# A re-planned order: the planner counts turns of the TensorE array and the SyncE time of transposing DMAs

## The chip, the cores and the metric

One core of one Trainium2 chip runs the whole program in one launch. The metric is the time on the device in microseconds (us). Engines: PE (TensorE, matmul), DVE (VectorE), ACT (ScalarE), POOL (GpSimd) and SP (SyncE, which here issues every DMA).

## The reference

Causal attention over 4 batches, 12 heads, 448 tokens and 64 channels per head, and behind it a two-layer MLP with a squared ReLU over all 1792 tokens. All inputs and outputs are float32.

```python
scores = (1/8) * q @ k.T                 # [4, 12, 448, 448], above the diagonal -1e9
attn   = exp(scores - max) / (sum + 1e-9)
x      = (attn @ v) as [1792, 768]       # tokens by heads*channels
out    = relu(x @ w_in)**2 @ w_out       # w_in [768, 2048], w_out [2048, 768]
```

## The kernel before, in words

**Stages.** Heads go in pairs, six pairs to a batch; two heads fill the 128 channels of PE's rows. For each pair PE transposes q and k (L570), then makes the scores in four passes c = 0 to 3 of 112, 224, 336 and 448 columns, one matmul per head and pass (L594; 64 of the array's 128 rows for each head, so both heads use the array side by side: the array is *split*). DVE adds the mask and takes the row maximum (L599), ACT makes the exponentials and their sums (L603). Batch 0 is turned by PE and multiplied in float32 (L629, L641). In batches 1 to 3 (pairs 0 to 17 below) the probabilities are divided by their sum and written as two halves in float16, a high one (L397 on ACT, L399 on DVE or POOL) and the remainder (L410 on DVE; L413 and L415, two instructions, on POOL), four pieces a head, into `psrc`. There is one `psrc` per head of the pair. A transposing DMA per head turns `psrc` into `pT` (L556), and PE multiplies `pT` with v in 24 matmuls for the pair (L651, split again, by columns): the *values*. They alternate between the two heads, so all but the first wait for both heads' DMA.

**MLP.** Tokens go in eight blocks of 128 or 256. Each block has a first layer of 16 groups of 18 matmuls (L918: three products of halves, six slices of 128 rows), then relu (L929), square (L936), high half (L397) and remainder (L405) of `g`, and a second layer (L954, 48 matmuls for each 128 tokens and 384 columns), scaled by ACT (L964) and stored by SP (L968). The 128-row matmuls use the *full* array. Weights are loaded, narrowed (L721 to L736) and split into halves (L397, L399, L410) while batch 0 runs.

**The order.** No engine's order is written by hand. `Plan.add` records each operation with the engines that may do it and their modelled durations, and with a due time made from the table `PR` (base, step and an offset by kind). `Plan.order` plays the program through once on the host: each time, the engine that can start first takes the ready operation with the earliest due time; an operation with several engines goes to the one that would end it first, `PR`'s bias included. The order that results is emitted, engine by engine, and each engine executes in that order and waits by semaphores. The model knows PE's clock (`warm`), the port that DVE and POOL share (`locks`), one DMA lane (`dma_free`), and how long SP is held by an issue (`ISSUE`: 475 ns, and 650 ns for a transposing DMA, `heavy`).

Of the kernel before, what the change touches and what calls it, by code (L numbers as in the profile page):

```python
# [18 lines left out]
E23 = float(2 ** 23)  # L19
PSC = float(2 ** 14)  # L20
PR = {
    "bias_dve": 329, "bias_act": -2161, "bias_pool": -229, "T0": -215719, "RAMP": 92933, "B1": 32241, "S1": 125326,
    "B2": 1585202, "S2": 69324, "B3": -4763872, "S3": 34284, "M0": 1770315, "RATE": 0.0019, "WI0": 135987,
    "WIR": 56308, "WS0": 3823057, "WSR": -44877, "WO0": 940458, "WOR": 183845, "WT0": -466469, "WTR": 280709,
# [5 lines left out]
    "m_L2": 2404805, "m_fac": -4350124, "m_ghi": 179886, "m_glo": -223927, "m_msq": 1943718, "m_ob": 5617141,  # L30
    "m_relu": -2665863, "m_sig": 3771052, "m_sq": -634180, "m_tau": 1847951, "wi_wl": 351942, "wi_wn": -1179075,
    "wi_wq": 1731582, "wo_wl": 2402465, "wo_wn": -983095, "wo_wq": -76879, "ws_wn": 4319096, "wt_wn": 1234225,
    "a0_P.copy@act": -2272, "a0_P.copy@dve": 3583, "a0_P.nrm@act": -308, "a0_P.nrm@dve": 3448, "a0_P.nrm@pool": -1037,
    "a0_qk.copy@act": -4902, "a0_qk.copy@dve": -890, "a0_x.top@act": 4549, "a0_x.top@dve": 5350,
    "m_ghi.hi@act": -5477, "m_ghi.hi@dve": -2320, "m_ghi.hi@pool": -5555, "m_glo.lo@dve": -384,
    "m_glo.lo@pool": -5962, "m_relu.@act": -4403, "m_relu.@dve": 5641, "m_sq.@act": -2058, "m_sq.@dve": 782,
    "m_sq.@pool": -1987, "ws_wn.hi@act": -3852, "ws_wn.hi@dve": -6000, "ws_wn.hi@pool": -3283, "ws_wn.lo@dve": -212,
    "ws_wn.lo@pool": 3600, "wt_wn.hi@act": -2079, "wt_wn.hi@dve": -3096, "wt_wn.hi@pool": -1467,
# [10 lines left out]
}  # L49


# [14 lines left out]
class Plan:  # L66
    LAT = {"pe": 197.0, "dve": 150.0, "act": 145.0, "pool": 90.0, "sp": 0.0}
    OWN = {"pe": 0.0, "dve": 127.0, "act": 143.0, "pool": 90.0, "sp": 0.0}
    WINDOW = 4096 / 1.2
    ISSUE = {False: 475.0, True: 650.0}  # L70

    def __init__(self):
        self.ops = []
        self.heavy = set()
        self.last_w = {}
        self.last_r = {}
        self.rings = {}
        self.spots = {}
        self.port = []
        self.bias = []  # L80
        self.kind = []

# [62 lines left out]
    def order(self):  # L145
# [7 lines left out]
        free = {}  # L153
# [20 lines left out]
            if left[i] == 0:  # L174
                offer(i)
        done = 0
        warm, busy, edge = False, 0.0, self.WINDOW
        while done < n:
            best = None
            for strict in (True, False):  # L180
                for e, c in cand.items():
# [5 lines left out]
                    if e in ("dve", "pool"):  # L187
                        t = max(f, min(max(r, shared) if locks(i, e) else r for i, r in c.items()))
                    else:
                        t = max(f, min(c.values()))  # L190
# [22 lines left out]
            t, e, i = best  # L213
            dur = self.ops[i][0][e]
            start[i] = t
            on[i] = e
            if e == "sp":
                free[e] = t + self.ISSUE[i in self.heavy]
                s = max(dma_free, free[e] + 625.0)
                dma_free = s + dur  # L220
                end[i] = s + dur + 930.0
            else:
                if e == "pe":
                    while t >= edge:
                        warm = busy >= 0.68 * self.WINDOW or (warm and busy >= 0.41 * self.WINDOW)
                        busy, edge = 0.0, edge + self.WINDOW
                    if not warm:
                        dur *= 2.0
                    s = t
                    while t + dur >= edge:  # L230
                        busy += edge - s
                        warm = busy >= 0.68 * self.WINDOW or (warm and busy >= 0.41 * self.WINDOW)
                        s, busy, edge = edge, 0.0, edge + self.WINDOW
                    busy += t + dur - s
                free[e] = t + dur
                end[i] = t + dur
                if locks(i, e):
                    shared = t + dur - 140.0
# [35 lines left out]
def mm32_ns(n):  # L274
    return n / 0.6 + 6
# [7 lines left out]
def attention_relu2_kernel(  # L283
# [9 lines left out]
    nc = tc.nc  # L293
# [87 lines left out]
    gf = g.rearrange("p k h t -> p (k h t)")  # L381
    xf = xt[1].rearrange("p k h t -> p (k h t)")

    def one(e, ns, fn, reads, writes, due, heavy=False, port=False):
        i = plan.add({e: ns}, fn, reads, writes, due, port=port)
        if heavy:
            plan.heavy.add(i)
        return i

    def hi(n, out, in_, scale, reads, writes, due):  # L390
# [153 lines left out]
    def halves(n, src, rr, rkey, pT):  # L544
# [3 lines left out]
        for c in range(NCH):  # L548
# [4 lines left out]
            hi(w, lambda half=half: half(0), from_, lambda c=c: rr(c, c + 1), [(src, c), rkey], [pk + (c, 0)], due)  # L553
            lo(w, lambda half=half: half(1), from_, lambda c=c: rr(c, c + 1), lambda half=half: half(0),
               [(src, c), rkey, pk + (c, 0)], [pk + (c, 1)], due, [(src, c)])
        one("sp", 2500, lambda e: nc.sync.dma_start_transpose(out=pT.ap, in_=ps.rearrange("p a d -> p (a d)")),  # L556
            [pk + (c, z) for c in range(NCH) for z in range(2)] + ["pads"], [pT], due, True)

    def pair(i):
        b, pr = divmod(i, NPAIR)  # L560
# [24 lines left out]
        for c in range(NCH):  # L585
# [7 lines left out]
                    r = slice(j * D, (j + 1) * D)  # L593
                    nc.tensor.matmul(out=ss[j].ap[0:P, 0:w], lhsT=q32.ap[r, c * P:w], rhs=k32.ap[r, 0:w], start=True, stop=True)  # L594

            one("pe", mm32_ns(w) + 95, scores, [q32, k32], ss, due)
            for j in range(2):
                s, due = ss[j], ("a", 2 * i + j + 0.05 * c, "sc")
                one("dve", dve_ns(w, 1, 1) - 10, lambda e, c=c, w=w, s=s, j=j: nc.vector.tensor_tensor_reduce(  # L599
# [55 lines left out]

        due = ("a", 2 * i + 1, "val")
        if b:
            one("pe", 1600, values16, [(vp, 0), (vp, 1)] + pT, [pv], due)
        else:
            one("pe", 2050, values, raws[2][1] + [(p_, a) for p_ in pT for a in range(0, NB10, 4)], [pv], due)  # L660
        due = ("a", 2 * i + 1, "x")
        o = 64 * (b % 2)
        xs = xt[b % 2][:, pr]
# [387 lines left out]
```

## Time and profile before

| what | us |
|---|---|
| median of 3 runs | 713.72 (710.70 to 714.43) |
| the profiled execution | 715.77 |
| its span, first to last instruction | 714.0 |
| PE busy | 658.6 (92% of the span) |
| ACT, DVE, POOL busy | 423.7, 325.8, 266.9 |

The profiled execution took 715.77 us by the device's own time, 1.8 us more than its span; it lies 0.3% above the median of the runs. All stretches and rows below are from this one execution, in microseconds from its start. Busy shares are means over stages with different limits, so they are read by stage in what follows.

### The profile page before, as it was taken

What the parts mean: (1) busy time and instruction counts of PE and PEld (TensorE: products, weight loads), DVE (VectorE), ACT (ScalarE), POOL (GpSimd) and SP (SyncE); (2) the same over time, 40 slices, a digit from 0 to 9 for tenths busy, and PEclk for the clock granted to TensorE, in tenths of its full rate; (3) what the DMA queues carried; (4) which work ended last, traced back from release to release, by engine and by line L of the source; (5) the groups of instructions that cost most, each with busy time, mean ns of one, the idle gap of its engine ahead of it and who ended that gap; (6) DMA issues with size and microseconds to landing.
All of it is one profiled execution on the core that took longest, in us unless ns stands there. A gap on an engine that the chain in (4) does not pass through costs nothing.

```text
span 714.0 us, 13829 instructions
## 1 busy us (share of the span) xinstructions
PE 658.6 (92%) x5182; PEld 465.0 (65%) x5182; DVE 325.8 (46%) x933; ACT 423.7 (59%) x1211; POOL 266.9 (37%) x382
## 2 busy tenths in 40 slices
PE   5877776799999899999999999999989899999998
PEld 3554544587666666787757756767656778776864
DVE  4999799889884555316320235123633110200000
ACT  2788978789876774774546664348645524414410
POOL 4232333215410326468348654447545202202200
PEclk9876767689999999999999999999999899999999
DMA  9997767545476664443365345435451300000000
GB/s 249 290 279 283 262 236 264 133 91 110 86 134 135 135 125 99 96 85 81 80 127 115 66 97 108 85 59 98 96 96 47 61 2 12 12 12 23 12 12 33
DMA packets 184866, 79.04 MB, mean 111 GB/s; under 512 B 173792, under 2 KB 179680, under 8 KB 184800
## 3 DMA queue, kind: packets, MB, share of 16 engines
q1 hardware_dynamic: 184800, 78.17, 45.7%
q8 instruction: 40, 0.66, 0.4%
q14 instruction: 26, 0.21, 0.1%
HBM read 45.81 MB, written 5.51 MB: 72 GB/s over the span
## 4 chain that ended last, share of the span: by engine, by line
PE 66%; DVE 14%; DMA 9%; POOL 5%; issue 3%; ACT 2%; SPq 1%; POOLq 0%; ACTq 0%; DVEq 0%
PE bank L918 27%; PE bank L954 23%; DMA pT<-psrc 7%; PE bank L594 5%; PE bank L651 4%; DVE bank L599 3%; PE bank L570 2%; DVE wo L724 2%; POOL p L413 2%; POOL psrc L415 2%; PE bank L641 2%; DVE wi L724 1%; DMA xt<-in_moe_w_out_dram 1%; DVE psrc L410 1%; DVE wo L721 1%
## 5 line engine op out<-in xcount | busy, mean ns | idle before, releaser
L918 PE MATMUL bank<-xt,wi 128*128 128x256 f16 (+1 forms) x2304 | 235.5, 262 | 0.0
L954 PE MATMUL bank<-wo,g 128*128 128x384 f16 x1344 | 228.8, 326 | 0.0
L918 PEld LDWEIGHTS <-wi 128*128 128x128 f16 x2304 | 201.5, 99 | 36.6 <-issue 14.3
L954 PEld LDWEIGHTS <-g 128*128 128x128 f16 x1344 | 128.2, 98 | 89.9 <-issue 10.0
L405 POOL TENSOR_TENSOR g<-g,g 128x256 f16<-128x256 f32 (+1 forms) x128 | 82.0, 650 | 197.2 <-ACT g L397 101.7
L599 DVE CUSTOM_DVE_ANT_0 bank<-bank,mask 112x112 f32<-112x112 f32 (+1 forms) x192 | 82.3, 472 | 128.8 <-PE bank L594 126.7
L603 ACT ACTIVATE p<-bank,nm 112x112 f32<-112x112 f32 (+1 forms) x192 | 93.3, 491 | 65.8 <-DVE nm L599 38.4
L594 PE MATMUL bank<-kT,qT 64*112 64x112 f32 (+3 forms) x384 | 78.0, 464 | 7.4 <-ACT p L603 4.4
L929 ACT ACTIVATE r<-bank 128x256 f32<-128x256 f32 (+1 forms) x128 | 45.0, 354 | 58.9 <-PE bank L918 58.0
L964 ACT ACTIVATE ob<-bank,fac 128x384 f32<-128x384 f32 x28 | 16.2, 579 | 82.5 <-PE bank L954 82.4
L397 ACT ACTIVATE psrc<-p,nm 112x448 f16<-112x448 f32 (+3 forms) x140 | 63.6, 524 | 0.4 <-ACT p L603 0.2
L415 POOL TENSOR_TENSOR psrc<-p,psrc 112x112 f16<-112x112 f32 (+3 forms) x76 | 53.8, 707 | 6.3
L936 ACT ACTIVATE g<-r 128x256 f32<-128x256 f32 (+1 forms) x122 | 46.8, 388 | 11.7 <-POOL g L405 7.0
L413 POOL TENSOR_SCALAR p<-p,nm 112x112 f32<-112x112 f32 (+3 forms) x76 | 43.5, 572 | 26.8 <-ACT psrc L397 26.8
L397 ACT ACTIVATE g<-g 128x256 f16<-128x256 f32 (+1 forms) x123 | 46.0, 386 | 10.7 <-PE bank L954 8.9
L594 PEld LDWEIGHTS bank<-kT,qT 64*112 64x112 f32 x384 | 31.4, 180 | 27.8 <-ACT p L603 10.9
L651 PE MATMUL bank<-pT,vp 112*64 112x336 f16 (+3 forms) x432 | 34.7, 295 | 12.2 <-DMA pT<-psrc 12.2
L410 DVE SCALAR_TENSOR_TENSOR psrc<-p,nm,psrc 112x336 f16<-112x336 f32 (+3 forms) x68 | 37.7, 592 | 10.5 <-ACT psrc L397 7.0
L651 PEld LDWEIGHTS <-vp 112*64 112x64 f16 x432 | 24.6, 114 | 24.3 <-issue 19.6
L603 ACT ACTIVATION_READ_ACCUMULATOR p<-bank,nm 112x1 f32 x192 | 38.1, 198 | 0.0
L736 POOL TENSOR_TENSOR wo<-wo,l 128x512 int32<-128x512 int32 (+1 forms) x16 | 20.0, 1253 | 44.3 <-DVE wo L724 9.2
L629 PE MATMUL bank<-ident,p 112*112 112x112 f32 x120 | 28.2, 394 | 6.2 <-ACT p L530 4.3
(120 smaller groups left out, 641.3 us busy)
## 6 DMA issues: line engine op xcount, KB each, us to landing
raw<-in_moe_w_out_dram SPq DMA_DIRECT2D x8, 768.0 KB, 5.1
xt<-in_moe_w_out_dram SPq DMA_DIRECT2D x8, 768.0 KB, 5.4
xt<-in_moe_w_in_dram SPq DMA_DIRECT2D x11, 512.0 KB, 6.2
out_dram<-ob SPq DMA_DIRECT2D x28, 192.0 KB, 2.0
raw<-in_moe_w_in_dram SPq DMA_DIRECT2D x9, 512.0 KB, 6.6
vn<-in_v_dram SPq DMA_DIRECT2D x18, 224.0 KB, 3.9
raw<-in_q_dram SPq DMA_DIRECT2D x36, 112.0 KB, 2.4
raw<-in_k_dram SPq DMA_DIRECT2D x36, 112.0 KB, 2.7
```

What stands on the lines that cost most here:

```text
L397: nc.scalar.activation(out=o, in_=i, func=ACTF.Copy, scale=s)
L405: return plan.add({"dve": dve_ns(n), "pool": pool2_ns(n)}, lambda e: engines[e].tensor_tensor(out=out(), in0=in_(), in1=top(), op=ALU.subt ...
L413: nc.gpsimd.tensor_scalar(out=in_(), in0=in_(), scalar1=scale(), scalar2=1.0, op0=ALU.mult, op1=ALU.mult)
L415: nc.gpsimd.tensor_tensor(out=out(), in0=in_(), in1=top(), op=ALU.subtract)
L594: nc.tensor.matmul(out=ss[j].ap[0:P, 0:w], lhsT=q32.ap[r, c * P:w], rhs=k32.ap[r, 0:w], start=True, stop=True)
L599: one("dve", dve_ns(w, 1, 1) - 10, lambda e, c=c, w=w, s=s, j=j: nc.vector.tensor_tensor_reduce(out=s.ap[0:P, 0:w], in0=s.ap[0:P, 0:w], in ...
L603: one("act", act_ns(w, True, 1, True), lambda e, c=c, w=w, b0=b0, s=s, j=j: nc.scalar.activation(out=p32[j].ap[:, b0:b0 + c + 1, :].rearra ...
L651: nc.tensor.matmul(out=pv.ap[j * D:(j + 1) * D, kc * P:S], lhsT=vp.ap[:, hv, vb:vb + D], rhs=pT[j].ap[0:P, hp * NSL + x:hp * NSL + x + w, ...
L918: nc.tensor.matmul(out=h.ap[:, 0:n], lhsT=wi_hl(ci, hw)[:, ms], rhs=x[:, kd, hx, off:off + n], start=(kd == 0 and hw == 0 and hx == 0), st ...
L929: nc.scalar.activation(out=r.ap[:, 0:n], in_=h.ap[:, 0:n], func=ACTF.Relu)
L936: nc.scalar.activation(out=g32.ap[:, 0:n], in_=r.ap[:, 0:n], func=ACTF.Square)
L954: nc.tensor.matmul(out=o.ap[:, 0:HALF], lhsT=g[:, kf, hg, tt * 128:(tt + 1) * 128], rhs=wo_hl(kf, hw)[:, hh * HALF:(hh + 1) * HALF], start ...
```

## The change

The table `PR` is replaced as a whole (all 150 numbers or so; two are shown), and the model that turns it into an order is changed in three places: a turn of the array between full and split use adds 93 ns, a transposing DMA holds SP for 3500 ns in place of 650 and its lane for 500 in place of 2500, and the values' modelled time is 1550 in place of 1600. What is computed, the tiles, and the buffers stay as they are.

```diff
-    "bias_dve": 329, "bias_act": -2161, "bias_pool": -229, "T0": -215719, "RAMP": 92933, "B1": 32241, "S1": 125326,
+    "bias_dve": 1722, "bias_act": -3826, "bias_pool": 4333, "T0": -530296, "RAMP": 129571, "B1": 324428, "S1": 232955,
...
-    ISSUE = {False: 475.0, True: 650.0}
+    ISSUE = 475.0
+    TURN = 93.0
...
-                free[e] = t + self.ISSUE[i in self.heavy]
+                free[e] = t + self.wait.get(i, self.ISSUE)
...
+                    if (i in self.tiled) != split:
+                        split = not split
+                        dur += self.TURN
...
-        one("sp", 2500, lambda e: nc.sync.dma_start_transpose(out=pT.ap, in_=ps.rearrange("p a d -> p (a d)")),
-            [pk + (c, z) for c in range(NCH) for z in range(2)] + ["pads"], [pT], due, True)
+        one("sp", 500, lambda e: nc.sync.dma_start_transpose(out=pT.ap, in_=ps.rearrange("p a d -> p (a d)")),
+            [pk + (c, z) for c in range(NCH) for z in range(2)] + ["pads"], [pT], due, 3500.0)
...
-            one("pe", mm32_ns(w) + 95, scores, [q32, k32], ss, due)
+            one("pe", mm32_ns(w) + 95, scores, [q32, k32], ss, due, tiled=True)
...
-            one("pe", 1600, values16, [(vp, 0), (vp, 1)] + pT, [pv], due)
+            one("pe", 1550, values16, [(vp, 0), (vp, 1)] + pT, [pv], due, tiled=True)
```

The new file has seven lines more from L80 on, so that L556 of before reads L563 after, L594 reads L601, L651 reads L658, L918 reads L925, L954 reads L961, L968 reads L975, and so on. Every engine's order is different from its first rows on. By kind, the counts of instructions differ in three ways: all 128 remainders of `g` (L405) go from POOL to DVE; of the 144 remainders of the probabilities POOL has 47 in place of 76, those of batches 1 and 2 being all on DVE and those of batch 3, but for one, on POOL; and of 18 remainders of v DVE has 16 in place of 3.

PE around the values of pair 16, the last but one: the matmuls, one row where equal kinds follow each other. Before:

```order
L594 MATMUL bank_119<-kT,qT 112x448
...
L918 MATMUL bank_131<-xt_147,wi 128x128
...
L954 MATMUL bank_143<-wo,g 128x384
...
L954 MATMUL bank_139<-wo,g 128x384
...
L594 MATMUL bank_119<-kT,qT 112x336
...
L651 MATMUL bank_115<-pT,vp 64x448
```

The same place of the change:

```order
L601 MATMUL bank_119<-kT,qT 112x448
...
L925 MATMUL bank_135<-xt_147,wi 128x256
...
L872 MATMUL bank_135<-sq,ones_b 128x128
...
L961 MATMUL bank_139<-wo,g 128x384
...
L925 MATMUL bank_131<-xt_147,wi 128x128
...
L601 MATMUL bank_119<-kT,qT 112x336
...
L658 MATMUL bank_115<-pT,vp 64x448
```

Between the last score pass of pair 16 and its values stood 72 matmuls of the first layer (128 columns), 54 of the second and three score passes of pair 17; now 36 of the first layer at 256 columns, 72 at 128, 48 of the second, seven small ones and the same three passes.

SP at the end of attention, from the transposing DMAs of pair 16 on (`psrc_150` and `psrc_151` are the two heads' `psrc`). Before:

```order
L556 DMA_TRANSPOSE pT<-psrc_150 128x26x112
L556 DMA_TRANSPOSE pT<-psrc_151 128x26x112
L968 DMA out_dram<-ob 128x384 x3
L556 DMA_TRANSPOSE pT<-psrc_150 128x26x112
L556 DMA_TRANSPOSE pT<-psrc_151 128x26x112
L968 DMA out_dram<-ob 128x384 x10
```

The same place of the change:

```order
L563 DMA_TRANSPOSE pT<-psrc_150 128x26x112
L975 DMA out_dram<-ob 128x384
L563 DMA_TRANSPOSE pT<-psrc_151 128x26x112
L975 DMA out_dram<-ob 128x384
L563 DMA_TRANSPOSE pT<-psrc_150 128x26x112
L975 DMA out_dram<-ob 128x384 x2
L563 DMA_TRANSPOSE pT<-psrc_151 128x26x112
L975 DMA out_dram<-ob 128x384 x10
```

Three stores stood ahead of both of pair 17's transposing DMAs; now two of them stand between the two.

POOL in pair 11 before, the second head's remainders (`p_4603` is that head's probabilities):

```order
L413 TENSOR_SCALAR p_4603<-p_4603,nm 112x336
L415 TENSOR_TENSOR psrc_151<-p_4603,psrc_151 112x3x112
L405 TENSOR_TENSOR g<-g_4748,g 128x256
L405 TENSOR_TENSOR g<-g_4754,g 128x256
L413 TENSOR_SCALAR p_4603<-p_4603,nm 112x448
L415 TENSOR_TENSOR psrc_151<-p_4603,psrc_151 112x4x112
```

POOL in pair 12 of the change, the first pair whose remainders are on POOL (`p_4482`, `p_4492`: its two heads):

```order
L420 TENSOR_SCALAR p_4482<-p_4482,nm 112x336
L422 TENSOR_TENSOR psrc_150<-p_4482,psrc_150 112x3x112
L420 TENSOR_SCALAR p_4482<-p_4482,nm 112x448
L422 TENSOR_TENSOR psrc_150<-p_4482,psrc_150 112x4x112
L420 TENSOR_SCALAR p_4492<-p_4492,nm 112x112
L422 TENSOR_TENSOR psrc_151<-p_4492,psrc_151 112x112
```

The `g` remainders that stood between a head's pieces on POOL have left it, and a pair's sixteen POOL instructions follow each other.

## Rows read from the trace of the kernel before

**Rows 1.** Windows, three stages: busy us (instructions) by engine, granted clock, DMA.

```profile
0.00:145.00 145.00, 105.51 (x630) 70.19 (x631) 126.25 (x337) 107.14 (x296) 47.09 (x41) 0.76 0.82 247
145.00:565.00 420.00, 407.60 (x3459) 287.64 (x3457) 190.41 (x572) 270.85 (x797) 197.86 (x307) 0.99 0.49 98
565.00:714.00 149.00, 145.50 (x1098) 107.12 (x1096) 9.14 (x26) 45.72 (x119) 21.97 (x34) 0.99 0.04 14
```

**Rows 2.** The tile pT: PE's idle time before it, SP's issues (ns), DMA to landing.

```profile
L556 SPq DMA_TRANSPOSE pT<-psrc x36: 3400/3534/4518, 158.2 to 553.9; - x36
...
  DMA pT<-psrc: 12.2, 9
...
DMA to landing us min/median/max: 5.3/5.5/7.3
```

**Rows 3.** Timeline of PE from pair 3's last score pass: start, us, instruction, [idle before].

```profile
213.35 1.01 PE L594 MATMUL bank<-kT,qT 64*112 64x448 f32 x4
...
218.18 2.18 PE L918 MATMUL bank<-xt,wi 128*128 128x128 f16 x36
220.20 0.33 PE L486 MATMUL bank<-s,ones_f 128*128 128x1 f32 x2
220.40 2.11 PE L954 MATMUL bank<-wo,g 128*128 128x384 f16 x12
222.35 0.55 PE L570 MATMUL bank<-ident,raw 112*128 112x112 f32 x4
...
228.26 0.38 PE L651 MATMUL bank<-pT,vp 112*64 112x448 f16 x1
229.34 1.59 PE L651 MATMUL bank<-pT,vp 112*64 112x448 f16 x23 [0.71 <-DMA pT<-psrc]
```

**Rows 4.** Timeline of SP in the same stretch: pair 3's two transposing DMAs.

```profile
220.26 7.12 SPq L556 DMA_TRANSPOSE pT<-psrc  x2
```

**Rows 5.** The chain of waits: start us, us, what; PE with and without turns.

```profile
300.35 13.86 PE bank L918 x126
...
314.77 2.07 PE bank L918 x18
...
321.22 0.94 PE bank L594 x4
```

**Rows 6.** Timeline of pair 11, whose remainders are all on POOL.

```profile
398.69 0.54 PE L594 MATMUL bank<-kT,qT 64*112 64x448 f32 x2
...
407.12 9.78 SPq L556 DMA_TRANSPOSE pT<-psrc  x2
...
410.43 1.30 POOL L405 TENSOR_TENSOR g<-g,g 128x256 f16<-128x256 f32 x2
...
420.67 1.59 PE L651 MATMUL bank<-pT,vp 112*64 112x448 f16 x23 [1.60 <-DMA pT<-psrc]
```

**Rows 7.** Timeline of pair 17, the last: stores and transposing DMAs on SP.

```profile
532.30 17.71 SPq L968 DMA_DIRECT2D out_dram<-ob  x3
...
549.08 0.58 ACT L964 ACTIVATE ob<-bank,fac 128x384 f32<-128x384 f32 x1 [5.98 <-PE bank L954]
...
550.17 7.38 SPq L556 DMA_TRANSPOSE pT<-psrc  x2
...
561.04 2.96 PE L651 MATMUL bank<-pT,vp 112*64 112x448 f16 x23 [2.65 <-DMA pT<-psrc]
```

**Rows 8.** Timeline of PE at pair 4's values, the second longest wait.

```profile
248.76 2.06 PE L651 MATMUL bank<-pT,vp 112*64 112x448 f16 x23 [1.87 <-DMA pT<-psrc]
```

**Rows 9.** Windows as in the first group: two stretches at a lower granted clock.

```profile
249.70:253.10 3.40, 3.40 (x25) 1.93 (x22) 1.54 (x3) 0.54 (x1) 1.56 (x2) 0.50 0.00 0
...
560.30:567.20 6.90, 6.16 (x55) 5.47 (x55) 1.25 (x2) 1.01 (x4) 0.03 (x1) 0.51 0.00 0
```

**Rows 10.** Remainders: groups by line and shape, xcount | busy us, mean ns | idle before.

```profile
L405 POOL TENSOR_TENSOR g<-g,g 128x256 f16<-128x256 f32 (+1 forms) x128 | 82.0, 650 | 197.2 <-ACT g L397 101.7
L410 DVE SCALAR_TENSOR_TENSOR psrc<-p,nm,psrc 112x336 f16<-112x336 f32 x21 | 12.7, 609 | 4.5 <-ACT psrc L397 4.4
```

More of the change, by code (lines that the diff above doesn't have):

```diff
@@ L21 @@
 PR = {
-    "bias_dve": 329, "bias_act": -2161, "bias_pool": -229, "T0": -215719, "RAMP": 92933, "B1": 32241, "S1": 125326,
-    "B2": 1585202, "S2": 69324, "B3": -4763872, "S3": 34284, "M0": 1770315, "RATE": 0.0019, "WI0": 135987,
-    "WIR": 56308, "WS0": 3823057, "WSR": -44877, "WO0": 940458, "WOR": 183845, "WT0": -466469, "WTR": 280709,
[5 rows of a table removed]
-    "m_L2": 2404805, "m_fac": -4350124, "m_ghi": 179886, "m_glo": -223927, "m_msq": 1943718, "m_ob": 5617141,
-    "m_relu": -2665863, "m_sig": 3771052, "m_sq": -634180, "m_tau": 1847951, "wi_wl": 351942, "wi_wn": -1179075,
@@ L32 @@
[L32 to L36, printed above, removed]
@@ L37 @@
-    "m_sq.@pool": -1987, "ws_wn.hi@act": -3852, "ws_wn.hi@dve": -6000, "ws_wn.hi@pool": -3283, "ws_wn.lo@dve": -212,
-    "ws_wn.lo@pool": 3600, "wt_wn.hi@act": -2079, "wt_wn.hi@dve": -3096, "wt_wn.hi@pool": -1467,
[10 rows of a table removed]
+    "bias_dve": 1722, "bias_act": -3826, "bias_pool": 4333, "T0": -530296, "RAMP": 129571, "B1": 324428, "S1": 232955,
+    "B2": 812082, "S2": 41854, "B3": -4102098, "S3": 123719, "M0": 2419066, "RATE": 0.0003, "WI0": 134258,
+    "WIR": 78726, "WS0": 5086006, "WSR": -83416, "WO0": 836150, "WOR": 255051, "WT0": 245622, "WTR": 375654,
[5 rows of a table added]
@@ new lines @@
+    "m_L2": 2418415, "m_fac": -4274908, "m_ghi": 93655, "m_glo": 401615, "m_msq": 502235, "m_ob": 4971607,
+    "m_relu": -2275338, "m_sig": 3136493, "m_sq": 500977, "m_tau": 1794324, "wi_wl": 340814, "wi_wn": -666176,
+    "wi_wq": 1959221, "wo_wl": 4392746, "wo_wn": -815068, "wo_wq": 173085, "ws_wn": 4344692, "wt_wn": 1272941,
+    "a0_P.copy@act": 2377, "a0_P.copy@dve": 1036, "a0_P.nrm@act": 963, "a0_P.nrm@dve": -1258, "a0_P.nrm@pool": 186,
+    "a0_qk.copy@act": 1468, "a0_qk.copy@dve": -350, "a0_x.top@act": -2802, "a0_x.top@dve": -880,
@@ L49 @@
+    "m_ghi.hi@act": -3814, "m_ghi.hi@dve": -2028, "m_ghi.hi@pool": -564, "m_glo.lo@dve": 4251, "m_glo.lo@pool": 4849,
+    "m_relu.@act": -4940, "m_relu.@dve": 6000, "m_sq.@act": 384, "m_sq.@dve": -1001, "m_sq.@pool": 4274,
+    "ws_wn.hi@act": 3561, "ws_wn.hi@dve": 5165, "ws_wn.hi@pool": -4891, "ws_wn.lo@dve": -3664, "ws_wn.lo@pool": 1345,
+    "wt_wn.hi@act": -5969, "wt_wn.hi@dve": 1519, "wt_wn.hi@pool": -1383, "wt_wn.lo@dve": -3057,
[10 rows of a table added]
 }
@@ L69 @@
     WINDOW = 4096 / 1.2
-    ISSUE = {False: 475.0, True: 650.0}
+    ISSUE = 475.0
+    TURN = 93.0
     def __init__(self):
         self.ops = []
-        self.heavy = set()
         self.last_w = {}
@@ L79, in __init__ @@
         self.port = []
+        self.tiled = set()
+        self.wait = {}
         self.bias = []
@@ L176, in order @@
         done = 0
-        warm, busy, edge = False, 0.0, self.WINDOW
+        warm, busy, edge, split = False, 0.0, self.WINDOW, False
         while done < n:
@@ L382, in attention_relu2_kernel, with one @@
     xf = xt[1].rearrange("p k h t -> p (k h t)")
-    def one(e, ns, fn, reads, writes, due, heavy=False, port=False):
+    def one(e, ns, fn, reads, writes, due, wait=None, port=False, tiled=False):
         i = plan.add({e: ns}, fn, reads, writes, due, port=port)
-        if heavy:
-            plan.heavy.add(i)
+        if wait:
+            plan.wait[i] = wait
+        if tiled:
+            plan.tiled.add(i)
         return i
@@ L657, in pair @@
         if b:
-            one("pe", 1600, values16, [(vp, 0), (vp, 1)] + pT, [pv], due)
+            one("pe", 1550, values16, [(vp, 0), (vp, 1)] + pT, [pv], due, tiled=True)
         else:
-            one("pe", 2050, values, raws[2][1] + [(p_, a) for p_ in pT for a in range(0, NB10, 4)], [pv], due)
+            one("pe", 2050, values, raws[2][1] + [(p_, a) for p_ in pT for a in range(0, NB10, 4)], [pv], due, tiled=True)
         due = ("a", 2 * i + 1, "x")
```

30 rows, old and new, of the table PR are left out of this document.

## The prediction

> **What bounds the kernel now.** I read the windows by stage first. To 145 us PE is busy but cold (0.76 of its clock) and DVE is the engine without slack, 126.25 of 145 us [rows 1]: weights and batch 0 go through it, and no first-layer matmul can start before they are done. From 145 to 565 us PE is busy for 407.60 of 420 us at 0.99 of its clock while DVE has work for 45% and POOL for 47% [rows 1]; from 565 on PE alone works. So from 145 us on the time is PE's work plus PE's idle time plus what a lower clock costs, and a new order of the same matmuls can only touch the last two. Next I looked for who ends PE's idle time: the tile view of pT shows 12.2 us in nine waits, all for the transposing DMA [rows 2], which is nearly the whole 12.4 us that the second stage leaves PE idle. In the timeline each wait has one form: the values' first matmul runs, on head 0, and the second stands until head 1's DMA has landed [rows 3]. SP shows why: one such DMA holds it 3.5 us, so two issued together take 7.12 [rows 4], and the second lands 5.5 us behind its issue [rows 2]. The planner of before had SP free again after 0.65 us. Last, the clock: two stretches of 3.4 and 6.9 us ran at half of it, right behind the two longest waits [rows 7 to 9].
>
> **The values' waits.** Call *chain* what passes from the end of a pair's last score pass to the landing of its second transposing DMA, and *cover* the matmuls that stand between that pass and the values. A wait is chain less cover. Pair 3: the pass ends at 214.4, its DMAs go out at 220.3 and 223.9, the second lands at 229.3, a chain of 14.9; its values start at 228.3, a cover of 13.9 [rows 3, 4]. Read likewise, the six pairs of batch 1, with every remainder on DVE, have chains of 18.1, 18.1, 17.6, 14.9, 16.9 and 15.7 us; pairs 6 to 11, all on POOL, 19.4 to 23.5; pair 11 ends its pass at 399.2 and waits until 420.7, 21.4 us, with 1.3 us of two `g` remainders between its own pieces [rows 6]. Part of the spread is the landing: most take 5.5 us, some 7.1 [rows 2].
>
> The new covers I add up from the new order by rows of before: a first-layer matmul 0.110 us at 256 columns (13.86 by 126) and 0.056 at 128 (2.02 by 36), a second-layer one 0.163 (1.95 by 12), a score pass 0.94 at 448 columns and 0.19 less for each 112 fewer [rows 3, 5]. For pair 16: 36 x 0.110 + 72 x 0.056 + 48 x 0.163 + 1.7 (three passes) + 1.2 (small ones and turns) = 18.7, against 72 x 0.056 + 54 x 0.163 + 1.7 + 0.3 = 14.8 before, where the trace has 14.8. In the same way the new covers of pairs 0 to 17 are 18.7, 19.2, 16.8, 17.7, 17.4, 16.1, 15.9, 15.6, 17.2, 17.2, 17.2, 20.1, 18.7, 20.0, 23.1, 19.3, 18.7 and 26.7. They are more even than before's (13.9 to 33.2): in batch 1 and 2 most values now stand behind the next pair's last score pass, not ahead of it.
>
> Set against chains: pairs 0 to 2 keep their own (18.1, 18.1, 17.6), so 0.8 us is left at pair 2. Pairs 3 to 11, on DVE, have 14.9 to 16.9: no wait with a landing of 5.5, up to 1.3 us at pairs 5 to 7 with one of 7.1; I take 1.0 for the three. Pairs 12 to 16, on POOL, have pair 11's chain without the `g` pieces: 21.4 - 1.3 = 20.1, and 18.5 with a landing of 5.5. That leaves 0 to 3.7 us over five pairs; 1.8. Pair 17 is bound by SP, not by POOL. Before, three stores stood ahead of both its DMAs and held them until 550.17, for the store of a tile that ACT wrote at 549.08 [rows 7]. Now the first DMA goes ahead and only the second stands behind two stores: the last of them waits for PE's second-layer group that ends 7 us before the values, plus 1.1 us to the issue as in those rows and 5.5 to 7.1 for landing, so a wait of 0 to 1.2 in place of 2.65; 0.6. Sum 4.2 in place of 12.2: **-8.0** (from -12.2 to -3.4).
>
> **The clock.** The two slow stretches cost 1.7 us (3.4 at half) and 3.0 (6.9 less some 0.8 in which PE waited, at half) [rows 9]. Ahead of them PE had stood for 1.87 and 2.65 us, the two longest waits [rows 7, 8]; pair 11's 1.60 [rows 6] was followed by none. With the longest waits gone I take **-3.2**, between -4.7 and nothing.
>
> **Turns.** Eighteen first-layer matmuls take 2.07 us where a turn stands at their end and 1.98 (18 x 0.110) where none does [rows 5]: 0.09 us a turn. By my count of the two orders the turns are 166 before and 172 now, and 138 and 142 from the first MLP matmul on. So in spite of the model's new term this part is **+0.4**, as ahead of the MLP PE is not the limit. The Trainium skill bears on it: TensorEngine Tiling (Array Packing), Key Properties, says that changing the tiling mode, not merely the tile, drains the array; the trace agrees that a turn costs, and by that rule alone the change would lose the same 0.4 us.
>
> **The first 145 us.** DVE has 329 instructions up to the last rescale that the first MLP matmul needs, where it had 331: two weight operations and two tiny ones fewer, two copies more, about 1 us less in all; on the other side PE has made eight transposes fewer by then (0.1 us each) and makes them later. **-0.5**, between -2 and +1, since DVE's 18.75 us of idle time there [rows 1] may shift either way.
>
> **The start of the second layer.** The output weights' scale comes 42 DVE instructions behind that rescale, where it came 10 behind. The first second-layer matmuls stand behind eight groups of the first layer (8 x 18 x 0.110 = 15.8 us) and some 5 us of other matmuls, 21 us; their weights stand behind 53 DVE instructions, 17.6 us at that stage's mean (190.41 by 572) [rows 1], and more with DVE's waits. Cover and cost nearly meet: **+1.5**, from 0 to +4.
>
> **The move of the `g` remainders** costs nothing in itself: on POOL 128 took 82.0 us [rows 10]; on DVE a remainder of 336 columns takes 0.61 [rows 10], one of 256 by columns alone 0.46, and I take 0.52, 50 us for the 96 wide ones and some 12 for the narrow, into the 230 us in which DVE stood idle from 145 to 565 us [rows 1]. If that cover fails, it is the second rival. The tail has PE busy throughout and the same matmuls: 0.
>
> Sum: -8.0 - 3.2 + 0.4 - 0.5 + 1.5 = -9.8 us. The profiled execution took 715.77 with a span of 714.0, so the next would take 706; as it lay 2 us above the median of 713.72, the median goes to **704 us**. All terms at their better ends give 695, all at their worse ends 715.6.
>
> **Rivals.** *The waits change places (710 to 715, 712 as its middle).* Batch 3 puts all sixteen POOL instructions of a pair in one row, and DVE now works beside them on `g`. If POOL's pieces are held up by 1.3 us a pair, as much as the two `g` pieces cost pair 11 [rows 6], the chain is 20 to 21.4 against covers of 18.7 to 20.0, 5 to 7 us over four pairs; with the clock's 1.5 at best and 4 us at the start of the second layer, little is left of the gain. For it: the POOL pairs of before had the longest chains. Against: none of them waited on `g` from another engine. The Trainium skill speaks for it: SBUF — State Buffer, Who interferes with whom, has a DVE instruction with two SBUF inputs and a POOL instruction that reads SBUF shut each other out for the whole instruction; the `g` remainder is one. No row above sets these two side by side, and the 1.3 us is not taken from it.
>
> *DVE is held by the `g` remainders (718 to 725, slower).* POOL stood 101.7 us of its 197.2 us ahead of L405 waiting for ACT's high half [rows 10], which cost nothing on POOL. On DVE the row maxima and the probabilities' remainders are queued behind such a wait, and PE's next score pass and the transposing DMA wait for those. 60 waits of 1.7 us are some three a pair; if one of them falls into each pair's chain, 18 x 1.7 = 30.6 us meet 16 us of slack (covers less chains, pair by pair, at most 1.7 each), so 14 us of new waits beside the 4.2, 6 us over the 12.2 of before; with the clock as before and +1.4 for the rest, 721. It decides from about 1.2 us a pair, where the waits are back at 12.2. Against it: DVE has more than half of that stage free, and the pieces of one head follow each other on DVE without a `g` between them.
>
> **Chances.** The forecast (699 to 709.5) 0.60; better, with an earlier end of the first stage as well (under 699), 0.05; the first rival 0.23, a tenth of it under 710; the second 0.12. A measurement of this kernel tells 0.5% from no change, 710.2 to 717.3: faster 0.67, same 0.21, slower 0.12. For 8 in 10 the range takes in the forecast and nearly all of the first rival: 699 to 715; the forecast's own is 699 to 709.5.
>
> **What would show it.** PE's idle time for pT near 4 us, the rest of it at pairs 12 to 17; values 16 to 20 us behind their pair's last score pass; no slow clock between 150 and 650 us, or one short stretch; first-layer matmuls from 143 to 145 us on. The forecast is wrong if the pT waits stay above 8 us, if `L599` on DVE starts late behind L412 (the `g` remainder's new line) with PE idle ahead of its score passes, or if PE idles ahead of the first L961.

## The result, and the profile after

The changed kernel takes 696.59 us, median of four runs (694.99 to 696.91), where the kernel before takes 713.09 (710.70 to 714.43): a ratio of 0.9768, 95% interval 0.9736 to 0.9799. The direction and the mechanism are those of the forecast; the gain is 16.5 us in the medians where 9.7 were forecast, and the time lies 2.4 us below the range's lower end. Timed twice more beside the kernel before, it gained 13.0 and 14.9 us (698.56 and 697.53 us, both below the range too). The profiled executions, 696.91 with a span of 695.2 against 715.77 with 714.0, lie further apart (18.9 us), as the one of before was among its slower ones; the account below is between these two. Starts of the MLP that are not in a row are counted from the first instruction of a computing engine, 0.3 us less than on the timelines.

Windows by stage come first, as in [rows 1]: busy us (instructions) of PE, PE's weight loads, DVE, ACT, POOL, granted clock, DMA share, GB/s; the last row is the stretch from the first stage's end to the end of the matmuls.

```profile
0.00:145.00 145.00, 104.80 (x631) 69.06 (x632) 121.72 (x336) 103.00 (x286) 49.02 (x44) 0.79 0.80 241
145.00:565.00 420.00, 417.87 (x3618) 297.84 (x3617) 229.26 (x723) 281.40 (x824) 83.14 (x129) 1.00 0.50 100
565.00:695.20 130.20, 126.64 (x937) 91.41 (x935) 16.64 (x44) 38.54 (x100) 0.00 (x0) 1.00 0.05 16
145.20:694.00 548.80, 544.30 (x4552) 389.09 (x4550) 245.90 (x767) 319.94 (x924) 82.94 (x129) 1.00 0.40 80
```

In the middle stage PE is idle for 2.13 us of 420, where it was 12.40, and the granted clock is 1.00 from 145.2 to 694 us: both stretches of [rows 9] are gone. The tile pT and PE's waits answer to [rows 2]: one wait for a transposing DMA is left of nine (three more, of 0.1 us each, are too short for these lists). The DMAs themselves are as before, 3.56 us on SP and 5.4 to landing.

```profile
L563 SPq DMA_TRANSPOSE pT<-psrc x36: 3398/3560/4423, 156.4 to 537.2; - x36
...
  DMA pT<-psrc: 1.5, 1
...
DMA to landing us min/median/max: 5.2/5.4/7.4
```

```profile
PE bank L658 <- DMA pT<-psrc: 1.5, 1, 1.5
PE bank L601 <- ACT p L610: 0.4, 1, 0.4
```

PE's timeline (start, us, instruction, idle before it) shows three more things.

```profile
142.46 3.43 PE L925 MATMUL bank<-xt,wi 128*128 128x256 f16 x18
...
163.78 2.12 PE L961 MATMUL bank<-wo,g 128*128 128x384 f16 x12
165.84 0.38 PE L658 MATMUL bank<-pT,vp 112*64 112x448 f16 x1
167.67 1.59 PE L658 MATMUL bank<-pT,vp 112*64 112x448 f16 x23 [1.45 <-DMA pT<-psrc]
169.19 0.82 PE L601 MATMUL bank<-kT,qT 64*112 64x336 f32 x4
...
543.02 1.62 PE L658 MATMUL bank<-pT,vp 112*64 112x448 f16 x24
544.57 3.64 PE L925 MATMUL bank<-xt,wi 128*128 128x128 f16 x62
```

The first matmul of the MLP starts at 142.46, 2.16 us earlier than the 144.62 of before. The second layer starts without a wait. And the values of pair 17 pass in one piece and hold PE for 544.57 - 543.02 = 1.55 us, while those of pair 0, broken by a wait, hold it for 169.19 - 165.84 - 1.45 = 1.90 besides the wait. A broken block holds PE 0.35 us longer, which no list of waits shows. It is not a cost beside the wait but the rest of it: pair 0's second DMA landed at 167.63, 1.79 us behind the values' start, and 1.45 + 0.35 = 1.80.

### The profile page after: what moved, and what is told of

Same layout as the page of the kernel before. It is cut to its first block, busy times and chain, and to the rows that moved or that the text cites. A ratio compares the mean times of both kernels' runs of the same rounds, so it can differ in the third digit from the quotient of the medians.

```text
span 695.2 us, 13690 instructions
## 1 busy us (share of the span) xinstructions
PE 649.3 (93%) x5182; PEld 458.3 (66%) x5182; DVE 367.6 (53%) x1103; ACT 422.9 (61%) x1210; POOL 132.2 (19%) x172
## 4 chain that ended last, share of the span: by engine, by line
PE 68%; DVE 12%; POOL 6%; DMA 5%; ACT 4%; issue 3%; SPq 1%; POOLq 0%; DVEq 0%; ACTq 0%
PE bank L961 26%; PE bank L925 26%; PE bank L601 6%; PE bank L658 4%; DMA pT<-psrc 3%; POOL psrc L422 3%; PE bank L577 2%; POOL p L420 2%; DVE bank L606 2%; DVE wo L731 2%; ACT p L610 1%; DMA vn<-in_v_dram 1%; DVE wi L731 1%; PE bank L648 1%; PE bank L636 1%
## 5 line engine op out<-in xcount | busy, mean ns | idle before, releaser
L925 PE MATMUL bank<-xt,wi 128*128 128x256 f16 (+1 forms) x2304 | 233.5, 260 | 0.0
L961 PE MATMUL bank<-wo,g 128*128 128x384 f16 x1344 | 226.3, 326 | 0.0
L925 PEld LDWEIGHTS <-wi 128*128 128x128 f16 x2304 | 199.4, 98 | 32.8 <-issue 11.4
L961 PEld LDWEIGHTS <-g 128*128 128x128 f16 x1344 | 129.8, 98 | 85.9 <-issue 4.4
L412 DVE TENSOR_TENSOR g<-g,g 128x256 f16<-128x256 f32 (+1 forms) x128 | 50.3, 410 | 148.0 <-ACT g L404 93.8
L601 PE MATMUL bank<-kT,qT 64*112 64x112 f32 (+3 forms) x384 | 75.5, 458 | 6.8 <-ACT p L610 4.3
L971 ACT ACTIVATE ob<-bank,fac 128x384 f32<-128x384 f32 x28 | 16.1, 579 | 93.8 <-PE bank L961 86.9
L404 ACT ACTIVATE psrc<-p,nm 112x112 f16<-112x112 f32 (+3 forms) x116 | 53.6, 523 | 0.1
L601 PEld LDWEIGHTS bank<-kT,qT 64*112 64x112 f32 x384 | 30.0, 178 | 28.0 <-ACT p L610 10.9
L417 DVE SCALAR_TENSOR_TENSOR psrc<-p,nm,psrc 112x336 f16<-112x336 f32 (+2 forms) x97 | 44.6, 504 | 6.6 <-ACT psrc L404 6.5
L636 PE MATMUL bank<-ident,p 112*112 112x112 f32 x120 | 31.0, 403 | 17.6 <-ACT p L537 13.4
L420 POOL TENSOR_SCALAR p<-p,nm 112x112 f32<-112x112 f32 (+3 forms) x47 | 25.9, 550 | 101.2 <-DVE psrc L406 101.2
L636 PEld LDWEIGHTS bank<-ident,p 112*112 112x112 f32 x120 | 19.2, 198 | 28.3 <-ACT p L537 21.2
L422 POOL TENSOR_TENSOR psrc<-p,psrc 112x112 f16<-112x112 f32 (+3 forms) x47 | 34.6, 736 | 3.9
L406 POOL TENSOR_SCALAR psrc<-p,nm 112x336 f16<-112x336 f32 (+1 forms) x8 | 4.7, 596 | 153.9 <-DVE nm L620 121.2
L658 PE MATMUL bank<-pT,vp 112*64 112x112 f16 (+3 forms) x432 | 30.8, 284 | 1.8 <-DMA pT<-psrc 1.5
```

Of the source, the lines that this page charges most:

```text
L404: nc.scalar.activation(out=o, in_=i, func=ACTF.Copy, scale=s)
L412: return plan.add({"dve": dve_ns(n), "pool": pool2_ns(n)}, lambda e: engines[e].tensor_tensor(out=out(), in0=in_(), in1=top(), op=ALU.subt ...
L417: nc.vector.scalar_tensor_tensor(out=out(), in0=in_(), scalar=scale(), in1=top(), op0=ALU.mult, op1=ALU.subtract)
L422: nc.gpsimd.tensor_tensor(out=out(), in0=in_(), in1=top(), op=ALU.subtract)
L636: nc.tensor.transpose(t.ap[0:P, (x - a) * P:(x - a + 1) * P], p32[j].ap[:, c * (c + 1) // 2 + kc, :], ident[0:P, 0:P])
L658: nc.tensor.matmul(out=pv.ap[j * D:(j + 1) * D, kc * P:S], lhsT=vp.ap[:, hv, vb:vb + D], rhs=pT[j].ap[0:P, hp * NSL + x:hp * NSL + x + w, ...
```

## The experiments

"Same chip" is said where kernels were timed together; the changed kernel, timed three times, gave medians of 696.59, 698.56 and 697.53; the last two are from one chip, which is the one meant. Theory A is the prediction's: a wait is chain less cover, and the covers carry the gain. Lines left out of an edit are marked by dots.

**Only one half of the change.** The new table in the old planner (the table PR swapped, nothing else):

```
-    "bias_dve": 329, "bias_act": -2161, "bias_pool": -229, "T0": -215719, "RAMP": 92933, "B1": 32241, "S1": 125326,
+    "bias_dve": 1722, "bias_act": -3826, "bias_pool": 4333, "T0": -530296, "RAMP": 129571, "B1": 324428, "S1": 232955,
...
```

> Half of the change: the new table of numbers in the planner of before. The shares of the engines come out as in the changed kernel (all g remainders on DVE, psrc remainders of pairs 0 to 11 on DVE, of 12 to 17 on POOL), the turns are ten fewer, but the covers are 2 to 4 us shorter at twelve pairs. Theory A (wait is chain less cover): the changed kernel's measured chains against these covers give waits of 4.2, 3.1, 2.6, 1.7, 1.9, 1.8, 1.7, 1.8, 1.3, 0.7, 2.9, 1.0 and 0.8 us, 25.5 in all, 3 us more for interrupted blocks, 0.9 less for turns, 2 to 10 for the clock: 722 to 734 us, slower than before. Theory B (the new shares of the engines carry the gain, the place of the values is a detail): 695 to 702 us.

Measured 728.38 us (728.00 to 734.00; ratio to before 1.0246, 1.0205 to 1.0286): slower than before, though the engines' shares are the changed kernel's. 15 of 18 values wait:

```profile
  DMA pT<-psrc: 18.5, 15
```

18.5 us where 25.5 were expected, with half-clock stretches of 3.4, 3.4, 10.2 and 3.4 us between 147 us and the end, which cost some 9 us. Theory B falls: with the same shares, and covers that are shorter at 13 of the 18 pairs, the kernel is 30 us slower than the changed one on the same chip.

The other half, the new planner with the old table:

> The other half of the change: the new planner with the table of before. The engines' shares stay as before (all g remainders on POOL, pairs 6 to 11 on POOL); turns 174. Theory A (chain less cover): the chains of before against these covers give waits of 2.1, 1.6, 9.4, 0.3, 0.3, 1.3 and 1.4 us at pairs 0, 2, 6, 7, 8, 11 and 12 and 0 to 9 at pair 17, 16 to 25 in all where before had 12.2; clock 2 to 10 us where it had 4.7: 716 to 735 us. Theory E (the better model orders the work better with any table): under 708 us.

Measured 715.03 us (711.87 to 718.62; ratio 1.0022, 0.9996 to 1.0048). It falls just short of theory A's 716 and far from theory E's 708, and the working behind the 716 was wrong: the pT waits did not grow, they went as low as in the changed kernel. PE's waits from 140 us on:

```profile
PE bank L601 <- ACT p L610: 6.0, 5, 4.2
PE bank L909 <- DVE u L902: 3.8, 2, 2.7
PE bank L658 <- DMA pT<-psrc: 1.4, 1, 1.4
```

Of the 10.8 us saved there, 8.7 came back as waits for ACT and DVE behind the MLP's start, and 3.4 as a later start of it (148.06 us on PE's timeline); 10.3 us ran at half clock, at the 2.7 and the 4.2, as much as in the kernel before. So it is the planner that sets the values' waits: 12.2 and 18.5 us with the one of before, 1.4 and 1.5 with the new one, each with the old and the new table. The time falls only where the table keeps the other engines ahead of PE too. Which of the planner's three changes does it, no run separates. My mistake was to carry chains of before over to another order: pair 6, priced at a wait of 9.4, waited 0.1, as its values were held up along with everything else.

**The covers put back.** In the changed kernel, eight pairs' values two PE operations earlier:

```
...
+        for pair, step in {2: -2, 4: -2, 5: -2, 6: -2, 7: -2, 8: -2, 9: -2, 10: -2}.items():
...
+            seq.insert(to, seq.pop(at))
```

> The changed kernel with the values of pairs 2 and 4 to 10 two PE operations earlier: ahead of the score pass they stood behind and of one step of the MLP, 1.9 to 2.9 us. Nothing else moves. Theory A (a wait is chain less cover, less 0.4 us that the first value matmul takes): shift less measured slack less 0.4 gives waits of 0.8 to 2.7 us, 14.0 in all; at pairs 5, 6, 8, 9 and 10 the values of the pair before no longer count in the cover, 1.55 us each, 7.8 in all; each interrupted block of values takes 0.35 us more, 2.3 in all. Sum 24 us, and 0 to 10 for lower clocks behind the longer waits: 721 to 731 us. Theory B (the engines' new shares shortened the chains so much that the place of the values hardly counts): under 702 us.

Measured 730.41 us (728.21 to 731.18; ratio 1.0243, 1.0211 to 1.0275), inside theory A's range, though its parts came out otherwise: the pT waits are 17.7 us in all, less than the sum had for them, and 7.0 us of waits for ACT and DVE, most of them ahead of the next transposes, were not in it. Three of its pT waits and the windows right behind them:

```profile
292.32 2.34 PE L670 MATMUL bank<-pT,vp 112*64 112x448 f16 x23 [2.69 <-DMA pT<-psrc]
...
317.45 2.96 PE L670 MATMUL bank<-pT,vp 112*64 112x448 f16 x23 [2.85 <-DMA pT<-psrc]
...
341.27 2.96 PE L670 MATMUL bank<-pT,vp 112*64 112x448 f16 x23 [2.03 <-DMA pT<-psrc]
```

```profile
292.70:296.40 3.70, 3.70 (x31) 2.92 (x27) 0.00 (x0) 0.00 (x0) 0.00 (x0) 0.54 0.02 4
316.90:323.80 6.90, 6.35 (x40) 4.69 (x40) 0.00 (x0) 0.00 (x0) 0.00 (x0) 0.51 0.00 0
340.80:347.70 6.90, 6.43 (x41) 4.74 (x40) 0.00 (x0) 0.00 (x0) 0.00 (x0) 0.51 0.00 0
```

With each wait come 3.4 to 6.8 us at 1.2 GHz, half of the full 2.4.

**SyncE's order at pair 17.** Its first transposing DMA behind the two stores again:

```
...
+        stores = [k for k in sp if k > turns[0] and cat(k) == "ob"][:2]
+        seq.insert(stores[1], seq.pop(turns[0]))
```

> The changed kernel with one step moved on SyncE: pair 17's first transposing DMA stands behind the two stores between the two, as in the kernel before. Theory A (SyncE's order alone made before's longest wait): the first goes out at 537.2 and the second 3.6 us later, lands 5.4 us behind that at 546.2, and PE, which reaches the values at 543.0, waits 2.8 us; 0.35 for the interrupted block, and nothing to 3.4 us for a lower clock behind it: 699 to 704 us. Rival (the second DMA waits for the stores in any case, so the first one's place is free): no new wait, 696 to 698 us.

Measured 702.94 us (701.65 to 706.09; ratio 0.9874, 0.9833 to 0.9915), 4.4 us over the changed kernel on the same chip. SP, then PE:

```profile
521.71 15.98 SPq L991 DMA_DIRECT2D out_dram<-ob  x3
537.86 7.28 SPq L579 DMA_TRANSPOSE pT<-psrc  x2
```

```profile
543.67 0.38 PE L674 MATMUL bank<-pT,vp 112*64 112x448 f16 x1
547.62 2.96 PE L674 MATMUL bank<-pT,vp 112*64 112x448 f16 x23 [3.57 <-DMA pT<-psrc]
```

That is [rows 7] made again: both DMAs go out together behind the last store, and PE waits 3.57 us, with 6.8 us at half clock. One place in SP's queue is worth a third of the gain on that chip (4.4 of 13.0 us).

**The `g` remainders on POOL.**

```
+            if self.ops[i][4][2] == "glo":
+                e = "pool"
```

> The changed kernel's order on every engine, but the 128 g remainders are POOL's again. Theory A (the gain is that each pair's values stand behind more matmuls than their chain lasts; the move of the g remainders is worth nothing in itself): POOL was idle in batches 1 and 2, so nothing changes there; in batch 3 the g pieces lie between POOL's own remainders as they did at pair 11, chains 1.3 us longer, which uses up the slack of pairs 12, 13, 15 and 16 (-0.5, -0.4, 0.7, 0.8 us): 3 us of new waits, 698 to 701 us. Theory B (the gain is the work taken off POOL): most of it is lost, 706 us or more. Theory C (DVE's added 50 us slow the chains, which hides part of the gain): 694 us or less.

Measured 703.52 us (702.88 to 705.45; ratio 0.9868, 0.9836 to 0.9899): between theory A's range and theory B's, with C excluded. The `g` pieces stand between POOL's own at pair 12, as at pair 11 in [rows 6], and PE waits there:

```profile
390.96 0.67 POOL L414 TENSOR_TENSOR g<-g,g 128x256 f16<-128x256 f32 x1
...
393.02 0.67 POOL L414 TENSOR_TENSOR g<-g,g 128x256 f16<-128x256 f32 x1
...
398.75 0.67 POOL L414 TENSOR_TENSOR g<-g,g 128x256 f16<-128x256 f32 x1
```

```profile
406.61 1.59 PE L660 MATMUL bank<-pT,vp 112*64 112x448 f16 x23 [1.54 <-DMA pT<-psrc]
```

Pair 12's chain is 20.5 us where the changed kernel has 19.1. The pT waits grew from 1.5 to 3.7, at pairs 12 and 13 (3 us more were expected, at four pairs); what I had not expected are 2.4 us of waits for ACT ahead of score passes, the longer of them (1.4 us, at pair 17) followed by a half-clock stretch. The changed kernel was not timed beside this one; against its three medians, taking `g` off POOL is worth 5 to 7 us, by the trace most of it in batch 3: theory A had the place, and half of the size.

**POOL's remainders of batch 3 on DVE.**

```
...
+            if phase == "a" and pos >= 36 and cat == "P" and e == "pool":
+                e = "dve"
```

> The changed kernel's order, with the probabilities' remainders of pairs 12 to 17 on DVE instead of POOL. Theory A: the chains of those pairs fall from 18.0 to 20.3 us to some 16 to 17, but only pairs 12 and 13 had a wait (0.1 us each and 0.35 for the block): 0.5 to 1.5 us less than the changed kernel, 695 to 697 us on this chip. Rival (DVE holds the row maxima or the g remainders up, PE waits ahead of score passes or second-layer groups): 700 us or more.

Measured 695.48 us (695.14 to 696.22; ratio 0.9758, 0.9733 to 0.9783), on the same chip as 697.53 of the changed kernel (696.57 to 699.10; 0.9788, 0.9760 to 0.9815). The chains of pairs 12 to 16 fell to 16.4, 16.6, 14.3, 15.5 and 16.6 us, pair 12's values pass whole:

```profile
381.76 1.01 PE L604 MATMUL bank<-kT,qT 64*112 64x448 f32 x4
...
401.43 1.62 PE L661 MATMUL bank<-pT,vp 112*64 112x448 f16 x24
```

This is the fastest kernel of the study and theory A held, but by little: the spans of the two profiled executions differ by 4.0 us, and 1.9 of that is an earlier start of the MLP, with the same instructions up to there. That it beats the changed kernel by more than the spread of starts is not settled.

**Filling the last waits.** Five blocks of values moved behind the next score pass:

```
...
+        for pair, step in {0: 4, 2: 3, 7: 3, 12: 1, 13: 1}.items():
...
+            seq[at:to + 1] = rest + late
```

> The changed kernel with the values of five pairs later: pair 0 behind two more groups of the first layer and one of the second, up to the next score pass (5.7 us), pairs 2 and 7 by 2.3 and 2.8 us up to the next score pass, pairs 12 and 13 behind one score pass; the turns of the array stay as many. Theory A (wait is chain less cover, and an interrupted block of values takes 1.90 instead of 1.55 us): the waits of 1.45, 0.10, 0.12 and 0.07 us go, and with them 0.35 us at pairs 0, 2, 12 and 13 and 0.23 at pair 7, 3.4 in all: 692.5 to 694.5 us, and under the changed kernel's time on the same chip. Theory D (these idle moments are hidden, what follows would wait as long elsewhere): 696 to 698 us.

Measured 699.77 us (699.39 to 701.93; ratio 0.9830, 0.9804 to 0.9855), 1.2 over the changed kernel on the same chip. PE's waits:

```profile
PE bank L590 <- DVE qT L559: 1.8, 2, 1.0
PE bank L614 <- ACT p L623: 1.6, 4, 0.7
PE bank L590 <- ACT qT L558: 0.9, 1, 0.9
PE bank L671 <- DMA pT<-psrc: 0.5, 1, 0.5
```

This is above both ranges. The mechanism is theory D's, and it costs more than D had: the four waits for DMAs are gone, one of 0.5 us is new, and 4.3 us of waits for ACT and DVE have come, as score passes and transposes now come before their inputs. The gentler form, one group of matmuls (the next of the first layer) drawn ahead of pair 0's values:

```
...
+        nxt = next(k for k in range(at, len(seq)) if self.ops[seq[k][0]][4][2] == "L1")
...
+        seq.insert(at, seq.pop(nxt))
```

> The changed kernel with one group of the first layer (18 matmuls, 1.98 us), the next in PE's own order, moved ahead of pair 0's values; the score pass between them stays where it was against DVE and ACT, and the turns stay as many. Theory A: pair 0's second DMA landed 1.8 to 2.3 us behind the values' start, so the wait of 1.45 to 1.92 us goes, with 0 to 0.35 for the interrupted block and, in executions where a lower clock followed that wait, 1.7 more: 1.5 to 3.9 us under the changed kernel on the same chip. Theory D (another wait takes its place, as when five blocks of values were put behind score passes): within 0.7 us of it.

Measured 696.88 us (695.28 to 697.69; ratio 0.9771, 0.9745 to 0.9798), 0.65 under the changed kernel on the same chip, within its spread: theory D again, if barely. Pair 0's wait is gone, and two others stand 10 and 20 us later:

```profile
167.50 1.91 PE L663 MATMUL bank<-pT,vp 112*64 112x448 f16 x24
...
177.73 0.60 PE L582 MATMUL bank<-ident,raw 112*128 112x112 f32 x4 [0.54 <-DVE qT L551]
...
188.31 0.63 PE L606 MATMUL bank<-kT,qT 64*112 64x224 f32 x2 [0.72 <-ACT p L615]
```

**The two stages exchanged.** The kernel before's first stage (all up to the first MLP matmul) with the changed kernel's rest, as a list of 770 operations ahead of the planner's:

```
...
+        done = {i for i, _ in seq}
+        seq += [(i, e) for i, e in self.order() if i not in done]
```

> Up to the first first-layer matmul the kernel of before's instructions and engines, from there the changed kernel's order. Theory A: it loses the 2.2 us of the start and keeps the waits' 10.3, the clock's 4.7 and the 2 us of uninterrupted values: 698 to 700 us. Theory C (the first stage carries the gain): 707 us or more.

Measured 697.84 us (697.56 to 698.99; ratio 0.9794, 0.9767 to 0.9821), just under theory A's 698, with one pT wait of 1.4 us. That is among the changed kernel's own three medians, so what its first stage is worth does not show in this total (the changed kernel was not timed beside it). The other way round:

> Up to the first first-layer matmul the instructions and engines of the changed kernel, from there the kernel of before's order. Theory A: the first stage is worth its 2.2 us earlier start and nothing more, the waits of the second stage stay: 709 to 712 us where the kernel before takes 713. Theory C (the first stage sets the clock and the waits behind it, the kernel gains by its better start): under 705 us.

Measured 725.32 us (724.08 to 727.51; ratio 1.0180, 1.0146 to 1.0214). This one is spoilt at the seam, where ACT's copy for a transpose stands too late in its queue:

```profile
155.13 1.01 PE L611 MATMUL bank<-ident,raw 112*128 112x112 f32 x4 [13.59 <-ACT qT L579]
```

Its total says nothing of the start. Its second stage does: eight pT waits of 10.5 us in all and two half-clock stretches, as in the kernel before. So the waits belong to the order of the second stage, not to what comes ahead.

**The changed kernel again,** twice on one chip, as the measure for the runs beside it:

> The changed kernel itself, to stand beside the others on one chip. 695 to 698 us; its first first-layer matmul within 140.5 to 144 us, since runs with the same instructions up to there started it at 140.9, 142.2 and 143.7 us.

> The changed kernel itself, for the same chip as the others: 695 to 700 us, pair 0's wait 1.4 to 2.0 us, a lower clock behind it in some of the executions.

698.56 us (695.07 to 699.39) and 697.53 us. In both profiles pair 0's wait was 1.92 us, with 3.4 us at half clock behind it, which the first profile, with 1.45, had not.

## Why the prediction was right in kind and too small

By its own steps, between the two profiled executions:

- *Values' waits, -8.0 forecast: -12.5 by the prediction's own measure.* The covers came out as added up: pair 12 at 18.7, pair 14 at 23.2 and pair 17 at 26.7, where 18.7, 23.1 and 26.7 stand on record, and none of eighteen more than 0.9 off. The chains came near theirs: 15.7 to 18.6 at pairs 1 to 11 (pair 3's 18.2 lies above the 16.9 given for its group), and 18.0 to 20.3 at pairs 12 to 16. Pair 0's alone was long, 20.4 for 18.1, and makes the one wait left; why, no run shows. The rule held as well, as time lost. In all profiles, 87 blocks of values at full clock had their second DMA land behind their start; in each, idle time and longer block together equal that lateness to 0.02 us (pair 3 of [rows 3]: the landing at 229.30 is 1.04 behind 228.26, PE idles 0.71 and the block is 0.35 longer).
- *The step that failed* is the subtraction "4.2 in place of 12.2". The 4.2 is chain less cover; the 12.2 of [rows 2] is idle time, which is counted from the end of the first value matmul and so is 0.34 us short of the time lost at each wait. By chain less cover the kernel before loses 15.8 us, at eleven pairs, and the changed one 3.3 (1.8 at pair 0, 0.2 to 0.5 at pairs 2, 7, 12 and 13). Of the 4.5 us that this term lacks, 3.6 lie in that starting point and 0.9 in the sizes. At the waiting pairs 1 to 5, 12, 16 and 17 the cover grew, by 0.8 to 4.9 us; at pair 11 it hardly did, and the chain fell from 21.4 to 15.7, with its remainders moved to DVE.
- *Broken blocks: -2.1, the part of the 12.5 that idle time (-10.4) leaves out.* Nine blocks of values were broken by a wait before, two more were longer without one; now four are broken and one is longer. At 0.35 us each this stood in [rows 3] too, had I added up the block on both sides of its wait. The kernel with the earlier values shows it again: 1.90 for every broken block at full clock.
- *The clock, -3.2: -4.7.* The forecast took away both of the longest waits and still kept a third of the price of the stretches behind them, as a middle between bounds. The two terms hang together: the slow stretches came with the longest waits. That all of it went is in part the luck of this execution: in the two other profiles of the changed kernel pair 0's longer wait brought 3.4 us at half clock back, and the term is -3.0, near the forecast.
- *The first stage, -0.5: -2.2.* DVE's last rescale ends 0.8 us earlier; the rest is PE's own queue, where 1.5 us of score pass, transposes and a small matmul stood between that rescale and the MLP and now stand elsewhere. I had priced DVE's queue, and of PE's only eight transposes, and those against the gain. The kernel before, then the changed one (the row of DVE is the rescale):

```profile
142.41 0.68 DVE L884 TENSOR_TENSOR xt<-xt,sg 128x1024 f16<-128x1024 f16 x1
142.00 1.46 PE L594 MATMUL bank<-kT,qT 64*112 64x336 f32 x4
143.39 0.58 PE L830 MATMUL bank<-s,ones_f 128*128 128x1 f32 x2
143.84 0.99 PE L570 MATMUL bank<-ident,raw 112*128 112x112 f32 x4
144.62 3.45 PE L918 MATMUL bank<-xt,wi 128*128 128x256 f16 x18
```

```profile
141.63 0.68 DVE L891 TENSOR_TENSOR xt<-xt,sg 128x1024 f16<-128x1024 f16 x1
```

  Nine executions with this first stage start the MLP at 140.1 to 143.7 us (mean 141.6), two with that of before at 143.4 and 144.3: the 2 us are in most, not in all.
- *The second layer's start, +1.5: 0.* Cover and cost met, as the text had it: of the two rows of output weights that the first twelve matmuls take, DVE ends the second one's remainder at 163.75, and PE starts the twelve at 163.78 without idling. It does not take the meeting to avoid a wait: in the third profile that remainder ends at 164.13, 0.44 us behind PE's start, and PE does not idle either. A term of nothing to 4 took its value from the middle; the row to look for was this one:

```profile
162.74 1.01 DVE L417 SCALAR_TENSOR_TENSOR wo<-wo,wst 128x768 f16<-128x768 f32 x1
```

- *Turns, +0.4:* the rest of the account, all idle time -10.3, blocks -2.1, clock -4.7, start -2.2, leaves +0.4 beside the 18.9. The trace has 138 turns before and 142 after, as counted; no run took a turn away alone.
- *The first rival* (POOL slowed by `g` on DVE) is real and small. POOL's scalings from 375 us to the end of attention, in the changed kernel and then with `g` on POOL (xcount, busy us, mean ns, idle):

```profile
L420 POOL TENSOR_SCALAR p<-p,nm 112x448 f32<-112x448 f32 x12 | 9.0, 754 | 0.0
L420 POOL TENSOR_SCALAR p<-p,nm 112x336 f32<-112x336 f32 x11 | 6.8, 619 | 0.0
```

```profile
L422 POOL TENSOR_SCALAR p<-p,nm 112x448 f32<-112x448 f32 x12 | 8.2, 681 | 0.0
L422 POOL TENSOR_SCALAR p<-p,nm 112x336 f32<-112x336 f32 x11 | 6.0, 548 | 0.0
```

  0.07 us a piece, 0.4 a pair over all pieces, against the 1.3 of the rival. The Trainium skill (SBUF — State Buffer, Who interferes with whom) has such pairs shut each other out for a whole instruction. DVE's `g` remainder takes 0.41 us, so by that rule most pieces met none.
- *The second rival* (DVE held by ACT's high half) did not come. DVE stood 93.8 us ahead of the `g` remainders for ACT, and PE waited 0.4 us ahead of score passes:

```profile
L412 DVE TENSOR_TENSOR g<-g,g 128x256 f16<-128x256 f32 (+1 forms) x128 | 50.3, 410 | 148.0 <-ACT g L404 93.8
```

Of the 9.1 us that the forecast lacks against the profiles, 3.6 are thus two measures in one subtraction, and 0.9 the sizes of the values' waits. The rest are three terms priced near the middle of their bounds, as if nothing tied them together, and each came out at its better end or just past it: the clock -4.7, the first stage -2.2, the second layer 0, where the better ends were -4.7, -2 and 0. Only the clock is tied to the waits by what these runs show; that the other two came out so well as well is luck as far as is known, and the two later timings, 1 to 2 us slower, show how much an execution can take back. (The worse ends add up to 715.7, not 715.6.)

## What to carry to other kernels

Where a consumer can start on one producer and needs another one's result soon after, the time lost is the later landing less the consumer's start. A list of idle time shows less of it, here 0.34 us less at each wait, so a modelled delay should not be set against measured idle time. Terms that hang on the same waits (idle, clock, longer blocks) are priced together, not each at its middle. And a last wait need not be worth filling: pushing the waiting block back moved what stands behind it ahead of its own inputs and cost 1.2 us in the medians; drawing one later group ahead of it took that wait away and brought others, 0.65 us better and within the spread.

## What the runs showed of the hardware that was not expected

All eight waits for a transposing DMA of 2.5 us or more in these profiles (2.56 to 3.57) came with 3.4 to 10.2 us at half clock, which began within 1.7 us of the wait's end, before or behind it. Of eleven waits between 1.77 and 2.05 us eight did; of ten between 1.43 and 1.63 us none, though one wait of 1.40 us for ACT did, with `g` on POOL. What else decides between these is not told apart here. And the first stage's end moves by 3.6 us between executions of the same instructions, while in three of the changed kernel what follows it, up to PE's last matmul, took 549.2, 550.9 and 551.5; what moves it was not tried.
